# Block-masked attention and two feed-forward layers on one core: three score tiles share a PSUM bank, and the planner of the instruction order judges by three clock moments

## The chip, the cores and the metric

The kernel is one launch on one core of a Trainium2 chip. The metric is the device time of that launch in microseconds (us), median of the runs shown. Five instruction streams run side by side and wait for each other by semaphores: PE (TensorE, matrix products), DVE (VectorE), ACT (ScalarE), POOL (GpSimd) and SP (SyncE, which here only issues DMAs). PSUM is the memory that PE writes its products to; it has eight banks, each of 512 float32 columns on 128 partitions.

## The reference

```python
def _attn_ref(q, k, v):                       # (4, 8, 576, 64), float32
    scores = 1/sqrt(64) * q @ k^T
    scores = where(query_block >= key_block, scores, -1e9)     # blocks of 64 tokens
    scores = scores - max(scores)
    attn = exp(scores);  attn = attn / (sum(attn) + 1e-9)
    return attn @ v

def _moe_ref(x, w_in, w_out):                 # 2304 x 512, d_ff 2048
    h = x @ w_in
    return (max(h, 0) + log1p(exp(-|h|))) @ w_out

def _moe2_ref(x, w_gate, w_val, w_out, rms_g):    # d_ff 1536
    xn = x / sqrt(mean(x * x) + 1e-6) * rms_g
    g = xn @ w_gate
    return (g * sigmoid(g) * (xn @ w_val)) @ w_out

def reference(...):  x = heads merged(attn);  x = _moe_ref(x);  return _moe2_ref(x)
```

## The kernel before

**Attention.** The work is cut into 48 *units* `u`: a batch `b`, a group `g` of 192 query tokens (three blocks of 64, `g` = 0, 1, 2) and a pair `p` of heads. Each unit has three *score tiles* `ib` = 0, 1, 2, one for each block of 64 queries of the two heads (128 rows), and `64 * (3g + ib + 1)` key columns wide, so that the mask costs nothing. For `g = 0`, a unit's first 192 tokens, the three tiles are 64, 128 and 192 columns wide. Units 0, 2, 4, 6, 12 to 15, 24 to 27 and 36 to 39 have `g = 0`, 16 in all. A score tile passes through this chain (`s_tile`, `s_exp`, `s_norm`, then `s_turn` or `s_split`): PE writes the scores into PSUM (L422), DVE takes the row maximum (L627), for the first 12 units scales it (L639), ACT takes the exponential with its row sum (L661), DVE makes the reciprocal of the sum (L669, L670), and the probabilities are normalised. In the first 12 units ("whole" units, float32 products) that is one instruction on POOL (L703), DVE (L704) or ACT (L705), then PE transposes the probabilities into PSUM (L716) and ACT (L722) or DVE (L723) copies them to SBUF. In the other units they are split into two float16 halves (L681 to L688) and a DMA transposes them (L693, `pt<-pst`). At last PE multiplies by v (`pv`), and ACT and DVE write the result as the feed-forward input `x`.

**Feed-forward.** The 2304 tokens are six blocks of 384. All products are in three passes of a split float32 (`PASSES`). `g1` and `g2` are the two products of the first layer, `g34` and `g5` those of the second. Until about 420 us the kernel interleaves attention with nine of the sixteen slices of the first layer for each block, and prepares weights on ACT, DVE and POOL (L448 to L461, L327, L337) as their DMAs land. The rest is feed-forward alone.

**PSUM.** `Banks` hands out whole banks: a score tile, a transposed tile, a `pv` result and a `g1` result each take one of the eight when they are first written and give it back when their last reader is done. `ring_a(u)` is the class from which score tiles and `pv` results come, with room for 4 banks at a time in the first units and 3 after that.

**The order.** Nothing is issued as it stands in the source. Each instruction is recorded by `Plan.op` with its engine, a duration, a key, and the cells that it reads and writes. `Plan.schedule` runs a list schedule with banks, DMAs and a model of PE's clock, whose two speeds change at moments of a fixed grid; `Plan.emit` repeats it with keys drawn towards the latest start of each instruction, keeps the best of 12 orders, and issues all instructions by their planned start. An instruction with alternatives (`aop2`, for instance a copy on ACT or DVE) gets its engine there. The semaphores are set afterwards by the tile layer below, from the tiles that the issued instructions touch, not by the plan.

## Time and profile before

| what | value |
|---|---|
| median of 3 runs | 1040.03 us (1039.77 to 1041.62) |
| the profiled execution | 1040.05 us, of which 1038.3 us span |
| PE, PEld busy | 1009.9 us (97%), 941.9 us (91%) |
| DVE, ACT, POOL busy | 667.8 us (64%), 580.1 us (56%), 214.0 us (21%) |
| the chain that ended last | PE 73%, DVE 9%, ACT 8%, DMA 7% |

The span is the time from the first to the last instruction of the execution that the profiler recorded; 1.75 us of its own time lie around it. PE's busy time includes its pipeline, so the free time of PE is what can be read, not how well its busy time is used. The busy shares are means over stages that differ: in the first 400 us DVE and ACT are busy for three quarters of the time or more, in the last 400 us for a quarter or less.

### The profile page before, as it was taken

How to read it: one execution, taken by the hardware profiler on the slowest of the kernel's cores; microseconds unless marked ns; L12 is line 12 of the kernel's file. 1: busy time of each engine (PE TensorE's matmuls, PEld its weight loads, DVE VectorE, ACT ScalarE, POOL GpSimd, SP SyncE). 2: the span in 40 equal slices, each digit the busy share in tenths (PEclk: the TensorE clock that was granted, in tenths of full speed). 3: DMA queues.
4: the chain of work that ended last, by engine and by line, in shares of the span. 5: the costliest groups of instructions: out<-in, count | busy, mean ns of one | idle time of the engine just before them, and what ended most of it. 6: DMA issues, size and time to landing. Idle time of an engine off the chain costs nothing.

```text
span 1038.3 us, 16885 instructions
## 1 busy us (share of the span) xinstructions
PE 1009.9 (97%) x6136; PEld 941.9 (91%) x6136; DVE 667.8 (64%) x1592; ACT 580.1 (56%) x1352; POOL 214.0 (21%) x289
## 2 busy tenths in 40 slices
PE   5999899999999999999999999999999999999998
PEld 4677898999989999999999999999999999999997
DVE  6899999887888677777888899422422423222322
ACT  6999798777778678877878664211211212111111
POOL 3543433331233023223324342000000000000000
PEclk9999999999999999999999999999999999999999
DMA  7454787958556635456444634200100100000000
GB/s 263 133 194 150 191 196 167 252 116 201 130 132 117 111 102 183 164 209 212 162 158 159 199 102 142 69 1 1 62 1 1 62 1 1 31 1 1 31 1 31
DMA packets 111635, 115.19 MB, mean 111 GB/s; under 512 B 84544, under 2 KB 92352, under 8 KB 110528
## 3 DMA queue, kind: packets, MB, share of 16 engines
q1 hardware_dynamic: 110976, 107.83, 36.8%
q0 software_dynamic: 576, 6.29, 1.6%
q8 instruction: 48, 0.79, 0.3%
q14 instruction: 35, 0.29, 0.1%
HBM read 72.03 MB, written 21.63 MB: 90 GB/s over the span
## 4 chain that ended last, share of the span: by engine, by line
PE 73%; DVE 9%; ACT 8%; DMA 7%; issue 2%; POOL 1%; SPq 0%; POOLq 0%; ACTq 0%; DVEq 0%
PE b L422 73%; DMA pt<-pst 4%; DMA wraw<-in_w_dram 2%; ACT P L661 1%; POOL wa L461 1%; ACT wa L448 1%; DVE wa L456 1%; DVE g L337 1%; ACT w L327 1%; DVE nm L627 1%; DVE wa L458 1%; DVE pst L686 1%; DVE t L836 1%; ACT t L834 1%; ACT P L705 1%
## 5 line engine op out<-in xcount | busy, mean ns | idle before, releaser
L422 PE MATMUL b<-x,w 128*128 128x384 f32 x2880 | 543.6, 338 | 2.0 <-DVE nm L669 0.8
L422 PEld LDWEIGHTS b<-x,w 128*128 128x128 f32 x2880 | 503.8, 188 | 13.8 <-issue 1.3
L422 PE MATMUL b<-g,w 128*128 128x384 f32 x1152 | 229.8, 339 | 2.2 <-DVE g L337 1.9
L422 PEld LDWEIGHTS b<-g,w 128*128 128x128 f32 x1152 | 199.4, 188 | 6.5 <-DVE g L337 3.6
L422 PE MATMUL b<-w,g 128*128 128x512 f32 x648 | 160.4, 392 | 0.0
L932 DVE TENSOR_TENSOR t<-b,t 128x384 f32<-128x384 f32 x72 | 40.0, 556 | 165.3 <-ACT t L931 165.1
L422 PEld LDWEIGHTS b<-w,g 128*128 128x128 f32 x648 | 120.6, 188 | 21.8
L461 POOL TENSOR_TENSOR wa<-wa,wraw 128x512 int32<-128x512 int32 x68 | 95.2, 1401 | 204.0 <-DVE wa L456 119.1
L931 ACT ACTIVATE t<-b 128x384 f32<-128x384 f32 x72 | 35.2, 490 | 171.8 <-PE b L422 171.8
L934 ACT CAST g<-t 128x384 fp32r<-128x384 f32 x72 | 36.8, 513 | 136.4 <-DVE t L933 136.4
L661 ACT ACTIVATE P<-b,nm 128x288 f32<-128x288 f32 (+8 forms) x160 | 80.1, 502 | 16.3 <-DVE nm L639 4.5
L627 DVE TENSOR_REDUCE nm<-b 128x1 f32<-128x288 f32 (+8 forms) x160 | 70.7, 447 | 18.7 <-PE b L422 17.6
L933 DVE TENSOR_TENSOR t<-b,t 128x384 f32<-128x384 f32 x72 | 39.9, 556 | 61.5 <-PE b L422 61.5
L686 DVE SCALAR_TENSOR_TENSOR pst<-P,nm,pst 128x128 f16<-128x128 f32 (+4 forms) x108 | 68.3, 638 | 9.1 <-ACT pst L683 6.7
L422 PE MATMUL b<-khl,qbd 128*128 128x448 f32 (+7 forms) x360 | 68.9, 312 | 1.0 <-ACT pt L722 1.0
L337 DVE TENSOR_TENSOR g<-t,g 128x384 fp32r<-128x384 f32 x96 | 60.5, 632 | 11.4 <-ACT g L327 10.9
L836 DVE SCALAR_TENSOR_TENSOR t<-b,t 128x384 f32<-128x384 f32 x96 | 52.6, 551 | 21.4 <-ACT t L835 21.0
L935 DVE TENSOR_TENSOR g<-t,g 128x384 fp32r<-128x384 f32 x72 | 42.9, 597 | 35.4 <-ACT g L934 35.4
L422 PEld LDWEIGHTS b<-khl,qbd 128*128 128x128 f32 x360 | 57.1, 188 | 3.9 <-ACT pt L722 1.2
L327 ACT CAST g<-t 128x384 fp32r<-128x384 f32 x96 | 49.2, 516 | 19.9 <-DVE t L836 16.8
L448 ACT ACTIVATE wa<-wraw 128x512 f32<-128x512 f32 x68 | 46.1, 678 | 20.9 <-DMA wraw<-in_w2gv_dram 10.7
L833 ACT ACTIVATE t<-b 128x384 f32<-128x384 f32 x96 | 46.5, 493 | 19.1 <-PE b L422 19.0
(91 smaller groups left out, 1055.7 us busy)
## 6 DMA issues: line engine op xcount, KB each, us to landing
wraw<-in_w_dram SPq DMA_DIRECT2D x32, 512.0 KB, 3.6
wraw<-in_w2gv_dram SPq DMA_DIRECT2D x24, 512.0 KB, 3.6
yd<-y SPq DMA_DIRECT2D x12, 768.0 KB, 3.7
y<-yd SPq DMA_DIRECT2D x12, 768.0 KB, 4.5
qf<-in_qP_dram SPq DMA_DIRECT2D x42, 192.0 KB, 2.8
xd<-x SPq DMA_DIRECT2D x4, 1536.0 KB, 7.1
x<-xd POOLq DMA_DIRECT2D x4, 1536.0 KB, 7.4
wraw<-in_w2o_dram SPq DMA_DIRECT2D x12, 512.0 KB, 4.4
```

Source lines behind the costliest of these rows:

```text
L327: "ACT": ("ACT", t_act(n), lambda: nc.scalar.copy(dst(), src())),
L337: "DVE": ("DVE", t_dve(n), lambda: nc.vector.tensor_tensor(dst(), a(), b(), ALU.subtract)),
L422: nc.tensor.matmul(o, lhsT=l, rhs=r, start=start, stop=stop)
L448: op("ACT", t_act(CW), prio, lambda a=a, hv=halves: nc.scalar.activation(a(), hv()[1].bitcast(FP32), ACTF.Abs), [raw], [a])
L461: op("POOL", t_pool2(CW), prio, lambda a=a, hv=halves: nc.gpsimd.tensor_tensor(a().bitcast(I32), a().bitcast(I32), hv()[0].bitcast(I32), A ...
L627: aop("DVE", t_dve(cn), key, lambda sp=sp, col=col, cn=cn: nc.vector.tensor_reduce(nm()[:, col:col + 1], sp()[:, :cn], axis=AX.X, op=ALU.m ...
L661: aop("ACT", 0.24 + cn * 0.836e-3, key, lambda sp=sp, col=col, c0=c0, cn=cn: nc.scalar.activation(P()[:, c0:c0 + cn], sp()[:, :cn], ACTF.E ...
L686: aop("DVE", t_dve(c, True), key, lambda: nc.vector.scalar_tensor_tensor(lo(), pc(), r(), hi(), ALU.mult, ALU.subtract), [P, (P, "pad"), ( ...
L833: op("ACT", t_act(BLK, False), key - 5, lambda: nc.scalar.activation(e(), h()[:, :BLK], ACTF.Abs), [h], [e])
L836: op("DVE", t_dve(BLK), key - 5, lambda: nc.vector.scalar_tensor_tensor(e(), h()[:, :BLK], 0.0, e(), ALU.max, ALU.add), [h, e], [e])
L932: op("DVE", t_dve(BLK), key + 2, lambda: nc.vector.tensor_tensor(u(), ga()[:, :BLK], u(), ALU.mult), [ga, u], [u])
L935: op("DVE", t_dve(BLK), key + 4, lambda: nc.vector.tensor_tensor(g()[:, 1], u(), g()[:, 0].bitcast(FP32), ALU.subtract), [u, (g, 0)], [(g, ...
```

## The change

Three things change. The three score tiles of a `g = 0` unit take one bank together, at columns 0, 64 and 192 (`o0`), where each took a bank of its own. The plan's cells are `(sp, ib)` for every score tile, so that for the plan the three parts of a bank are independent. And `emit` runs 24 rounds instead of 12, judges an order by the mean of its planned end over three places of the clock's grid (`PHASES`) instead of one, and goes on after a round that finds no order.

```diff
-    def schedule(self, key):
+    PHASES = (0.7, 1.8, 2.9)
+
+    def schedule(self, key, phase=PHASES[0]):
...
-                rest, share, dur, z = dur, self.cols[i] / dur, 0.0, t + 0.7
+                rest, share, dur, z = dur, self.cols[i] / dur, 0.0, t + phase
...
-        for r in range(12):
+        for r in range(24):
             try:
                 end, start, ends, bank, choice, eng, took = self.schedule(key)
             except TypeError:
-                break
-            if best is None or end < best[0]:
-                best = (end, start, bank, choice, key)
+                if best is None:
+                    raise
+                key = [(x + y) / 2 for x, y in zip(key, best[4])]
+                continue
+            try:
+                mean = (end + sum(self.schedule(key, p)[0] for p in self.PHASES[1:])) / len(self.PHASES)
+            except TypeError:
+                mean = INF
+            if best is None or mean < best[0]:
+                best = (mean, start, bank, choice, key)
...
+        o0 = (0, 64, 192)[ib] if g == 0 else 0
         for c0, cn in chunks:
-            sp = ring_a(u).new()
+            if g == 0 and ib:
+                sp = packed[u]
+            else:
+                sp = packed[u] = ring_a(u).new()
...
-                    mm(sp()[:, :cn], qt()[:, ib, :], k()[:, c0:c0 + cn], True, True)
+                    mm(sp()[:, o0:o0 + cn], qt()[:, ib, :], k()[:, c0:c0 + cn], True, True)
...
-            aop("PE", ..., key, qk, qr + kr, [sp], ...)
+            aop("PE", ..., key, qk, qr + kr, [(sp, ib)], ...)
...
-            aop("DVE", ... tensor_reduce(..., sp()[:, :cn], ...), [sp], [(nm, ib)])
+            aop("DVE", ... tensor_reduce(..., sp()[:, o0:o0 + cn], ...), [(sp, ib)], [(nm, ib)])
...
-            aop("ACT", ... activation(P()[:, c0:c0 + cn], sp()[:, :cn], ACTF.Exp, ...), [sp, (nm, ib)], ...)
+            aop("ACT", ... activation(P()[:, c0:c0 + cn], sp()[:, o0:o0 + cn], ACTF.Exp, ...), [(sp, ib), (nm, ib)], ...)
```

The whole order is drawn anew, on all engines. Three places follow. In the names `b_125` is a PSUM tile with its number, `y` and `raw` hold k, `qf` and `pst` hold q, `ones` is the identity for the transposes, `P` the probabilities, `nm` the small columns of maxima, sums and reciprocals, `wa` and `wraw` weights in preparation. Line numbers of the changed kernel are 9 to 14 higher (L422 is L431, L627 is L640, L716 is L730). A row ends with the semaphores that the instruction waits for, where they are asked for.

The first is the start of PE's stream with its waits, before (unit 0: 64, 128 and 192 columns; then the first two tiles of unit 1):

```order
L422 MATMUL b_125<-y,qf_107 128x64 [waits DMAHW1_49,DMAHW0_49]
L422 MATMUL b_129<-y,qf_107 128x128
L422 MATMUL b_135<-y,qf_107 128x192
L422 MATMUL b_143<-y,qf_108 128x256 [waits DMAHW2_49]
L422 MATMUL b_158<-y,qf_108 128x320
```

and in the changed kernel:

```order
L431 MATMUL b_125<-y,qf_107 128x64 [waits DMAHW1_49,DMAHW0_49]
L431 MATMUL b_125<-y,qf_107 128x128
L431 MATMUL b_125<-y,qf_107 128x192 [waits DVE_49]
L431 MATMUL b_141<-y,qf_108 128x256 [waits DMAHW2_49]
L431 MATMUL b_156<-y,qf_108 128x320
```

The order is the same, but the third product now waits for DVE: for the maximum of the first part, which reads the same bank. The second place is the start of DVE's stream with its waits, before:

```order
L627 TENSOR_REDUCE nm<-b_125 128x1 [waits PE_49]
L639 TENSOR_SCALAR nm<-nm 128x1 [waits DVE_49]
L627 TENSOR_REDUCE nm<-b_129 128x1 [waits PE_49]
L639 TENSOR_SCALAR nm<-nm 128x1 [waits DVE_49]
L669 TENSOR_SCALAR nm<-nm 128x1 [waits Activation_49]
L627 TENSOR_REDUCE nm<-b_135 128x1 [waits PE_49]
L670 RECIPROCAL nm<-nm 128x1 [waits DVE_49]
```

and in the changed kernel:

```order
L640 TENSOR_REDUCE nm<-b_125 128x1 [waits PE_49]
L652 TENSOR_SCALAR nm<-nm 128x1 [waits DVE_49]
L640 TENSOR_REDUCE nm<-b_125 128x1 [waits PE_49]
L652 TENSOR_SCALAR nm<-nm 128x1 [waits DVE_49]
L683 TENSOR_SCALAR nm<-nm 128x1 [waits Activation_49]
L640 TENSOR_REDUCE nm<-b_125 128x1 [waits Activation_49]
L684 RECIPROCAL nm<-nm 128x1 [waits DVE_49]
```

Again the order is the same; the third maximum now waits for ACT, whose exponentials of the first two parts read the same bank. The third place is PE's stream after the first six score tiles, before:

```order
L716 MATMUL b_198<-ones,P 128x128 x2
L422 MATMUL b_204<-y,pst 128x64
L716 MATMUL b_207<-ones,P 128x128 x2
L422 MATMUL b_212<-y,pst 128x128
L422 MATMUL b_215<-y,pst 128x192
L422 MATMUL b_228<-pt,pst 64x192 x2
L422 MATMUL b_228<-pt,pst 64x64 x2
L716 MATMUL b_257<-ones,P 128x128 x3
L716 MATMUL b_268<-ones,P 128x128 x3
L422 MATMUL b_275<-y,pst 128x256
L422 MATMUL b_284<-y,pst 128x320
L716 MATMUL b_297<-ones,P 128x128
```

and in the changed kernel:

```order
L730 MATMUL b_197<-ones,P 128x128 x2
L730 MATMUL b_204<-ones,P 128x128 x2
L431 MATMUL b_209<-y,pst 128x64
L730 MATMUL b_212<-ones,P 128x128 x3
L431 MATMUL b_219<-pt,pst 64x192 x2
L431 MATMUL b_219<-pt,pst 64x64 x2
L431 MATMUL b_209<-y,pst 128x128
L431 MATMUL b_209<-y,pst 128x192
L431 MATMUL b_235<-y,pst 128x256
L431 MATMUL b_240<-y,pst 128x320
L730 MATMUL b_251<-ones,P 128x128 x3
L730 MATMUL b_282<-ones,P 128x128
```

The transposes of unit 1's second tile (`b_257`, now `b_212`) stand ahead of unit 0's `pv`, and four score products of units 2 and 3 stand between that `pv` and the transposes of unit 1's third tile (`b_268`, now `b_251`). Elsewhere the new order differs in the same manner, by a few matmul groups. Over the first 12 units ACT has two more normalisations of 128x192 (L705), one more of 128x256 and of 128x64, one fewer of 128x320, and in copies of transposed tiles (L722) three fewer of 128x512, two fewer of 128x128 and one more of 128x384.

## Rows read from the trace of the kernel before

**Rows 1.** Windows by stage: busy time of each engine, PEclk, DMA share, GB/s.

```profile
4.38:25.00 20.62, 14.21 (x68) 10.63 (x68) 16.80 (x64) 14.84 (x45) 8.70 (x16) 0.92 0.82 286
25.00:100.00 75.00, 69.97 (x423) 55.26 (x423) 67.67 (x200) 71.60 (x185) 34.89 (x53) 1.00 0.49 157
100.00:420.00 320.00, 312.99 (x2358) 294.07 (x2357) 269.74 (x779) 252.93 (x647) 92.92 (x158) 1.00 0.66 158
420.00:1033.00 613.00, 612.11 (x3291) 581.75 (x3291) 312.90 (x551) 238.87 (x476) 77.08 (x57) 1.00 0.22 74
```

**Rows 2.** Waits of PE from 4 to 25 us: total us, times, longest.

```profile
PE b L716 <- ACT P L705: 3.7, 1, 3.7
PE b L422 <- ACT pt L722: 1.4, 1, 1.4
PE b L716 <- DVE P L704: 1.3, 1, 1.3
```

**Rows 3.** Windows of one us around the fall of PE's clock.

```profile
16.00:17.00 1.00, 0.03 (x1) 0.03 (x1) 1.00 (x9) 0.65 (x2) 1.00 (x1) 0.98 1.10 370
17.00:18.00 1.00, 1.00 (x5) 1.00 (x6) 1.00 (x5) 1.00 (x4) 0.34 (x1) 0.50 1.03 396
20.00:21.00 1.00, 1.00 (x4) 0.70 (x4) 0.64 (x4) 1.00 (x4) 0.77 (x2) 0.81 0.27 107
```

**Rows 4.** Timeline of unit 0's maxima and exponentials: start, us, engine, line.

```profile
5.52 0.31 ACT L661 ACTIVATE P<-b,nm 128x64 f32<-128x64 f32 x1 [3.50 <-DVE nm L639]
5.61 0.29 DVE L627 TENSOR_REDUCE nm<-b 128x1 f32<-128x128 f32 x1
...
6.25 0.36 DVE L627 TENSOR_REDUCE nm<-b 128x1 f32<-128x192 f32 x1
...
6.83 0.42 ACT L661 ACTIVATE P<-b,nm 128x192 f32<-128x192 f32 x1 [0.25 <-DVE nm L639]
...
8.35 1.49 PE L422 MATMUL b<-y,qf 128*128 128x384 f32 x2
```

**Rows 5.** Timeline of the events that the new order moves, 12 to 24 us.

```profile
12.15 0.39 ACT L722 COPY pt<-b 128x256 f32<-128x256 f32 x1
...
16.97 1.54 PE L716 MATMUL b<-ones,P 128*128 128x128 f32 x6 [3.71 <-ACT P L705]
...
21.48 1.09 PE L422 MATMUL b<-pt,pst 128*64 128x192 f32 x12
...
23.50 0.62 ACT L661 ACTIVATE P<-b,nm 128x384 f32<-128x384 f32 x1
```

**Rows 6.** ACT's groups by shape, first 100 us: count, busy us, mean ns, idle before.

```profile
L722 ACT COPY pt<-b 128x512 f32<-128x512 f32 x10 | 6.1, 609 | 0.0
L722 ACT COPY pt<-b 128x384 f32<-128x384 f32 x7 | 3.5, 496 | 0.7 <-PE b L716 0.7
L705 ACT ACTIVATE P<-P,nm 128x320 f32<-128x320 f32 x4 | 2.3, 578 | 0.9 <-DVE nm L669 0.9
L722 ACT COPY pt<-b 128x128 f32<-128x128 f32 x8 | 2.1, 266 | 1.0 <-PE b L716 1.0
L705 ACT ACTIVATE P<-P,nm 128x256 f32<-128x256 f32 x1 | 0.5, 548 | 0.0
L705 ACT ACTIVATE P<-P,nm 128x192 f32<-128x192 f32 x1 | 0.5, 461 | 0.0
L705 ACT ACTIVATE P<-P,nm 128x64 f32<-128x64 f32 x1 | 0.4, 351 | 0.0
```

**Rows 7.** Waits of PE from 25 to 100 us.

```profile
PE b L716 <- ACT P L661: 1.0, 2, 0.6
...
PE b L422 <- ACT P L661: 0.6, 1, 0.6
```

**Rows 8.** Waits of PE from 100 to 420 us.

```profile
PE b L422 <- DMA pt<-pst: 2.9, 5, 0.9
...
PE b L422 <- ACT P L661: 0.6, 2, 0.3
```

More of the change, by code (lines that the diff above doesn't have):

```diff
@@ L590, in small @@
         aop2([e[k] for k in kind], key, reads, writes, False)
-    part = {}
+    part, packed = {}, {}
     def s_tile(u, ib, key, after):
@@ L616, in qk @@
                 if whole(u):
-                    mm(sp()[:, :cn], qt()[:, ib, :], k()[:, c0:c0 + cn], True, True)
+                    mm(sp()[:, o0:o0 + cn], qt()[:, ib, :], k()[:, c0:c0 + cn], True, True)
                     return
                 for m, (a, c) in enumerate(PASSES):
-                    mm(sp()[:, :cn], d[:, a, ib, :], khl[p][:, c, c0:c0 + cn], m == 0, m == 2)
+                    mm(sp()[:, o0:o0 + cn], d[:, a, ib, :], khl[p][:, c, c0:c0 + cn], m == 0, m == 2)
             if c0 == 0:
                 qk_op.append(len(plan.ops))
-            aop("PE", max(0.213, 0.006 + cn * 1.667e-3) if whole(u) else 3 * t_mm(cn), key, qk, qr + kr, [sp], after=after, cols=t_mm16((4 if whole(u) else 3) * cn))
+            aop("PE", max(0.213, 0.006 + cn * 1.667e-3) if whole(u) else 3 * t_mm(cn), key, qk, qr + kr, [(sp, ib)], after=after, cols=t_mm16((4 if whole(u) else 3) * cn))
         for c, (sp, (c0, cn)) in enumerate(zip(bank, chunks)):
             col = ib + c
-            aop("DVE", t_dve(cn), key, lambda sp=sp, col=col, cn=cn: nc.vector.tensor_reduce(nm()[:, col:col + 1], sp()[:, :cn], axis=AX.X, op=ALU.max, negate=True), [sp], [(nm, ib)])
+            aop("DVE", t_dve(cn), key, lambda sp=sp, col=col, cn=cn: nc.vector.tensor_reduce(nm()[:, col:col + 1], sp()[:, o0:o0 + cn], axis=AX.X, op=ALU.max, negate=True), [(sp, ib)], [(nm, ib)])
         if len(chunks) == 2:
@@ L654, in s_exp @@
         nm, done = part[u]
+        o0 = (0, 64, 192)[ib] if units[u][1] == 0 else 0
         P = part[u, ib] = R_P.new()
@@ L660, in s_exp @@
             col = 4 + ib + c
-            aop("ACT", 0.24 + cn * 0.836e-3, key, lambda sp=sp, col=col, c0=c0, cn=cn: nc.scalar.activation(P()[:, c0:c0 + cn], sp()[:, :cn], ACTF.Exp, scale=scale, bias=nm()[:, ib:ib + 1], accum_out=nm()[:, col:col + 1]), [sp, (nm, ib)], [P, (nm, "s", ib)])
+            aop("ACT", 0.24 + cn * 0.836e-3, key, lambda sp=sp, col=col, c0=c0, cn=cn: nc.scalar.activation(P()[:, c0:c0 + cn], sp()[:, o0:o0 + cn], ACTF.Exp, scale=scale, bias=nm()[:, ib:ib + 1], accum_out=nm()[:, col:col + 1]), [(sp, ib), (nm, ib)], [P, (nm, "s", ib)])
         if len(chunks) == 2:
```

## The prediction

> **What bounds the kernel now.** I read the windows by stage first, to see where PE is free at all [rows 1]. From 420 us to 1033 us PE idles 613.00 - 612.11 = 0.9 us, so that nothing that an order does there can show. From 100 to 420 us it idles 320.00 - 312.99 = 7.0 us, with DVE busy for 84% and ACT for 79%. From 25 to 100 us it idles 75.00 - 69.97 = 5.0 us, and there ACT is busy for 71.60 of 75.00 us: that stretch goes at ACT's pace. From the first product at 4.38 us to 25 us it idles 6.4 us. So at most some 19 us, 1.9% of the time, can be won, and only by an order under which PE waits less; the amount of PE's work is the same before and after. I then read who ends PE's waits in each stretch. Early it is three single waits, 3.7, 1.4 and 1.3 us, all for one tile's chain of maximum, exponential, normalisation and copy [rows 2]. Behind the longest of them PE's granted clock shows 0.50, the lower of its two levels, 1.2 of 2.4 GHz: 0.98 in the slice from 16 us, 0.50 at 17, 0.81 in the slice from 20, so (1 - 0.98)/0.5 + 3 + (1 - 0.81)/0.5 = 3.4 us at half speed, a loss of 1.7 us of work [rows 3]. Later the waits are many and small, the largest group 2.9 us in five for transposing DMAs [rows 8].
>
> **The change, part by part.** The first thing is what the shared bank does to the issued waits, since the plan takes the three parts as independent and the tile layer below does not: the third product of unit 0 now waits for the first maximum, the third maximum for two exponentials, as the order's rows with their waits show, and the exponentials in turn wait for the maxima issued ahead of them. I follow unit 0 by hand with the durations of before.
>
> Before, the second maximum starts at 5.61 us and the third at 6.25 [rows 4]. Now the first maximum can start only when the second product is done, at 5.61; it takes 0.22 (0.29 and 0.36 for 128 and 192 columns, 0.07 for each 64), the third product follows at about 5.9, and since it can no longer overlap the second one I give it 0.85 to its reader where the rows show 0.64 between the readers. The second maximum then runs at 6.75 to 7.04, the first exponential at 7.1 instead of 5.52, the second to about 7.95, the third maximum at 8.0, and after its scaling the third exponential at 8.7 instead of 6.83. The transposes of the first two tiles, which stand ahead of the 384-column product in PE's stream, go with them: that product starts at 9.6 instead of 8.35. **The new waits cost PE 1.25 us at this point.**
>
> Then the new order gains it back. The copy that the first `pv` waits for starts at 12.5 instead of 12.15 [rows 5]. The six transposes that were held until 16.97 are parted: three of them (unit 1's second tile, now normalised on POOL) are done ahead of that `pv`, the score products of units 2 and 3 fill 1.5 us of the hole, and the other three start at about 16.3. Unit 1's `pv` starts at about 20.9 instead of 21.48. So PE is about 0.6 us ahead there. ACT is not: going on through its new order, the 384-column exponential of unit 3 starts at about 25.2 instead of 23.50, and of these 1.7 us only 0.461 + 0.351 = 0.8 us are normalisations that it has done earlier than before [rows 6]. As the next stretch goes at ACT's pace, the bounds are -0.6 (PE's lead is kept) and +1.7 (ACT's lag lands on PE); I take **+0.4**, between the lead and the true lag of 0.9. The clock: my chain still leaves PE idle from 15.0 to 16.3 and from 16.8 to 19.7, so I expect the lower level once more, a little later, at the same price: 0, with -1.7 as the bound if it does not fall.
>
> From 25 to 100 us ACT's load changes by the engine choices. Normalisations: 2 x 0.461 + 0.548 + 0.351 - 0.578 = +1.24 us. Copies: -3 x 0.609 - 2 x 0.266 + 0.496 = -1.87 us [rows 6]. Two of the normalisations are counted above, so 1.87 - (1.24 - 0.81) = 1.4 us less remain for this stretch; the copies go to DVE, which is busy for 67.67 of 75 us [rows 1] and takes most of that room away. I take **-0.5**, bounds -1.4 and 0.
>
> Units 4 and 6 have shared banks in this stretch too. Their order is three products, three maxima, three exponentials, so the first exponential waits for two more maxima, 0.29 + 0.36 = 0.65 us each [rows 4]. Other work may fill it: **+0.6**, bounds 0 and +1.3. The other twelve units stand after 100 us, where DVE is busy for 269.74 of 320 us and ACT for 252.93 [rows 1]. Each can lose about one exponential to a waiting maximum or the reverse, 0.42 [rows 4]; the room on both engines and the many matmuls that stand between a unit's scores and its `pv` cover it. I take **0**, bounds 0 and, if half of them show, 6 x 0.42 = +2.5.
>
> What the freed banks give: PE's waits that end with an exponential are those for a score bank to come free (the exponential is a score tile's last reader), 1.0 + 0.6 + 0.6 = 2.2 us [rows 7, 8]. A third of the score tiles are packed: **-0.7**, bounds -2.2 and 0. The new criterion redraws the order everywhere else; where the waits of 100 to 420 us fall next is open, and I take 0, bounded by the largest group, the transposing DMAs, gone or come twice, 2.9 us either way [rows 8]. Rounds and phases cost no instruction.
>
> Sum: 0.4 - 0.5 + 0.6 + 0 - 0.7 + 0 = -0.2 us on the profiled execution's own 1040.05 (1038.3 span and 1.75 around it), which lies 0.02 above the median of the runs shown: **1039.9 us**.
>
> A row of before cannot show two engines at one bank, since no two tiles share one there [rows 4]: maximum and exponential of neighbouring tiles overlap freely (the 128-column maximum starts 0.09 us after the 64-column exponential). The Trainium skill ("PSUM — Partial Sum Buffer", section "PSUM bank collisions raise a hardware error") says that two engines must be kept apart by bank and not by address, reads against reads included. By that rule the three parts never overlap on different engines in any of the 16 units, and the time would be that of the slower rival below; by the rows' overlap taken as still possible, that part of the sum would be 0.
>
> **The rivals.**
> *The shared bank costs more than the order gives.* Place: ACT in the first 100 us, ACT and DVE after that. All of ACT's lag lands on PE (+1.7), both of units 4 and 6 lose their 0.65 (+1.3), half of the later units 0.42 each (+2.5), and the lighter ACT gives its 0.5: 1040.05 + 5.0 = 1045.0. For it: the plan knows nothing of these waits, and ACT has 3.4 us of room in 75 [rows 1]. Against it: in the later units the maxima and exponentials are already issued nearly in sequence, and after 100 us both engines have room. It decides when over 2.6 of these 5.5 us land.
> *The early hole closes.* The three early waits are 6.4 us together [rows 2]; if the parted transposes halve them (-3.2) and the clock then stays up (-1.7): 1035.1. For it: more work stands in the hole. Against it: by my chain the hole only moves.
> *The banks were the limit.* All 2.2 us of bank waits go, and ACT's 1.4 us count in full: 1036.4. For it: ACT paces 75 us. Against it: the waits are five small ones, and an order kept under a looser rule need not spend the freedom there.
> *The change does nothing that shows*: gains and losses cancel; this is my forecast.
>
> **How the numbers follow.** A measurement of this kernel can tell about 0.2%, 2.1 us, from no change. Forecast, within 2.1 us: 0.42, with a range of its own of 1038 to 1042. Slower rival: 0.28. Early hole: 0.14. Banks: 0.16. The last two make 0.30 for faster. The range reaches over most of the three rivals: 1035.0 to 1045.3; about half of the early hole's cases and a third of the slower rival's lie outside, together some 0.17.
>
> **What would show it.** Right: the 64-, 128- and 192-column exponentials at about 7.1, 7.5 and 8.7 us; the 384-column product near 9.6; unit 1's `pv` between 20.5 and 21.5; a stretch at 0.50 as long as before, beginning a few us later; PE idle of about 5 us from 25 to 100 and 7 from 100 to 420. Wrong: exponentials of unit 0 near 5.5 to 6.9 (the bank costs nothing); no slice at 0.50 before 30 us; PE idle from 25 to 100 above 7 (slower) or below 3 (faster); new waits of PE's score products for DVE or ACT of over 1 us anywhere; waits for transposing DMAs far from 2.9 us, which would say that the new order and not the bank decides.

## The result, and the profile of the changed kernel

The changed kernel takes 1046.93 us (median of 6 runs, 1046.01 to 1050.08), the kernel before 1040.29 us (6 runs, 1039.19 to 1041.62). The ratio is 1.0065, interval 1.0052 to 1.0079: 6.6 us slower, and outside the predicted range. The profiled execution took 1046.88 us, of which 1045.0 us are span.

The windows by stage of the changed kernel, and below them its three stretches at half speed (columns as in [rows 1]):

```profile
4.38:25.00 20.62, 16.13 (x72) 10.64 (x74) 17.20 (x58) 14.91 (x46) 10.01 (x19) 0.83 0.80 283
25.00:100.00 75.00, 69.13 (x418) 54.94 (x415) 66.47 (x203) 68.56 (x174) 29.78 (x41) 0.95 0.45 151
100.00:420.00 320.00, 312.23 (x2328) 294.40 (x2327) 268.06 (x771) 249.03 (x645) 101.62 (x169) 0.98 0.67 158
420.00:1033.00 613.00, 611.26 (x3289) 581.58 (x3288) 319.25 (x552) 240.02 (x484) 86.24 (x63) 1.00 0.22 75
17.44:24.27 6.83, 5.14 (x23) 3.44 (x24) 6.49 (x24) 6.03 (x17) 4.12 (x8) 0.50 0.46 155
41.34:48.16 6.82, 6.07 (x24) 3.73 (x24) 5.97 (x23) 6.61 (x20) 1.64 (x4) 0.50 0.48 163
116.43:126.67 10.24, 8.71 (x48) 8.36 (x43) 7.51 (x36) 7.66 (x25) 3.86 (x9) 0.50 0.53 140
```

PE's idle time has hardly changed: 4.5 us (6.4 before), 5.9 (5.0), 7.8 (7.0) and 1.7 (0.9) by stage, 19.9 us against 19.3. What has grown is its busy time, 1016.5 us over the whole span against 1009.9, for the same products. Where it grew is in the last three rows: the granted clock shows 0.50 three times instead of once, and PE is busy in these stretches for 5.14 + 6.07 + 8.71 = 19.9 us, against 3.4 us before [rows 3]. Half of that is 10.0 us, against 1.7. The first reading is therefore that the clock is the loss. The experiments below show that most of the loss is something else.

Unit 0's chain came as it was worked out. ACT's and DVE's rows at its start (start, duration, and in brackets the idle time before, with what ended it) answer to [rows 4]:

```profile
7.22 0.31 ACT L675 ACTIVATE P<-b,nm 128x64 f32<-128x64 f32 x1 [5.19 <-DVE nm L640]
7.52 0.36 ACT L675 ACTIVATE P<-b,nm 128x128 f32<-128x128 f32 x1
8.58 0.42 ACT L675 ACTIVATE P<-b,nm 128x192 f32<-128x192 f32 x1 [0.61 <-DVE nm L652]
...
6.89 0.29 DVE L640 TENSOR_REDUCE nm<-b 128x1 f32<-128x128 f32 x1 [0.91 <-PE b L431]
8.00 0.36 DVE L640 TENSOR_REDUCE nm<-b 128x1 f32<-128x192 f32 x1 [0.20 <-ACT P L675]
```

The exponentials start at 7.22, 7.52 and 8.58 us (worked out: 7.1, 7.5, 8.7), the second maximum at 6.89 (6.75). No maximum and exponential of the unit run at the same time any more. That is what the rule of the Trainium skill ("PSUM — Partial Sum Buffer", section "PSUM bank collisions raise a hardware error") asks for, and the trace agrees with it; but here semaphores keep the two apart, so no run shows what the hardware would do without them.

PE's waits by stage (who was waited for; us in total, times, longest), which answer to [rows 2, 7, 8]: from 4 to 25 us, from 25 to 100 us, and from 100 to 420 us.

```profile
PE b L730 <- ACT P L719: 3.8, 2, 3.5
...
PE b L730 <- ACT pt L736: 2.2, 5, 0.7
PE b L730 <- ACT P L675: 1.2, 1, 1.2
...
PE b L431 <- ACT P L675: 0.7, 2, 0.5
...
PE b L431 <- DMA pt<-pst: 2.6, 3, 0.9
PE b L431 <- DVE x L797: 1.4, 1, 1.4
PE b L431 <- ACT khl L556: 1.2, 1, 1.2
PE b L431 <- ACT P L675: 1.0, 3, 0.7
```

The early hole has only moved (3.5 us for one normalisation instead of 3.7). From 25 to 100 us the transposes wait five times, 2.2 us in all, for ACT's copies of transposed tiles. Before, PE waited nearly as long for them there, 0.4 us ahead of a transpose and 1.6 ahead of other products:

```profile
PE b L422 <- ACT pt L722: 1.6, 3, 1.0
```

New near 120 us is a wait of 1.4 us for an addition of DVE (L797), and one of 1.2 us of a score product for ACT's part of k (L556).

### The profile page after: what moved, and what is told of

It is laid out like the page before. It is cut to its first block, busy times and chain, and to the rows that moved or that the text cites. A ratio compares the mean times of both kernels' runs of the same rounds, so it can differ in the third digit from the quotient of the medians.

```text
span 1045.0 us, 16874 instructions
## 1 busy us (share of the span) xinstructions
PE 1016.5 (97%) x6136; PEld 948.2 (91%) x6136; DVE 673.4 (64%) x1585; ACT 576.0 (55%) x1350; POOL 228.1 (22%) x298
## 4 chain that ended last, share of the span: by engine, by line
PE 73%; DVE 5%; DMA 4%; ACT 3%; issue 1%; POOL 1%; POOLq 0%; ACTq 0%; DVEq 0%; SPq 0%
PE b L431 73%; DMA pt<-pst 2%; DMA wraw<-in_w_dram 1%; DVE wa L465 1%; POOL wa L470 1%; ACT wa L457 1%; DVE wa L461 1%; ACT t L848 0%; DVE wa L467 0%; DVE t L850 0%; ACT w L336 0%; ACT g L336 0%; DMA wraw<-in_w2o_dram 0%; DVE g L346 0%; DMA wraw<-in_w2gv_dram 0%
## 5 line engine op out<-in xcount | busy, mean ns | idle before, releaser
L431 PE MATMUL b<-x,w 128*128 128x384 f32 x2880 | 545.6, 338 | 1.3 <-DVE x L767 0.5
L431 PEld LDWEIGHTS b<-x,w 128*128 128x128 f32 x2880 | 505.2, 188 | 12.5 <-ACT P L675 1.2
L431 PE MATMUL b<-g,w 128*128 128x384 f32 x1152 | 228.3, 340 | 0.4 <-DVE g L346 0.4
L431 PEld LDWEIGHTS b<-g,w 128*128 128x128 f32 x1152 | 200.3, 188 | 3.5 <-DVE g L346 0.6
L431 PE MATMUL b<-w,g 128*128 128x512 f32 x648 | 161.2, 393 | 0.0
L431 PEld LDWEIGHTS b<-w,g 128*128 128x128 f32 x648 | 120.6, 188 | 21.5
L640 DVE TENSOR_REDUCE nm<-b 128x1 f32<-128x288 f32 (+8 forms) x160 | 70.8, 450 | 23.4 <-PE b L431 18.5
L431 PE MATMUL b<-khl,qbd 128*128 128x448 f32 (+7 forms) x360 | 70.5, 319 | 2.6 <-ACT khl L556 1.2
L431 PEld LDWEIGHTS b<-khl,qbd 128*128 128x128 f32 x360 | 58.6, 196 | 5.9 <-ACT P L675 1.8
L847 ACT ACTIVATE t<-b 128x384 f32<-128x384 f32 x96 | 46.4, 489 | 18.4 <-PE b L431 18.1
```

Of the source, the lines that this page charges most:

```text
L431: nc.tensor.matmul(o, lhsT=l, rhs=r, start=start, stop=stop)
L640: aop("DVE", t_dve(cn), key, lambda sp=sp, col=col, cn=cn: nc.vector.tensor_reduce(nm()[:, col:col + 1], sp()[:, o0:o0 + cn], axis=AX.X, o ...
L847: op("ACT", t_act(BLK, False), key - 5, lambda: nc.scalar.activation(e(), h()[:, :BLK], ACTF.Abs), [h], [e])
```

## The experiments

Three theories at the start. **A, the clock:** the holes of the new order make it fall twice more, and half of the busy time at 0.50 is the loss. **B, the shared banks:** the waits between maximum and exponential cost the time themselves. **C, the order:** an order drawn anew is worse, with or without shared banks. One point needs no run. Built with the shared banks and the old criterion (12 rounds, one phase), the kernel has the same instructions in the same order on PE, DVE and ACT as the changed one. So the new criterion decides nothing here: the shared banks give the plan another order, and the old criterion finds the same one.

### Is it the clock?

Both kernels once more, unaltered.

> The changed kernel once more, nothing altered, for a second profile. The moments at which the granted clock can change stand at another distance from the first instruction in each execution. Theory A (half-speed stretches make the loss): again two or three stretches at 0.50 behind the holes near 17, 40 and 115 us, and a time that follows them: 1046 to 1050 us with 8 to 11 us of PE work lost or stretched, less only if a stretch is missing. Theory B (the waits at the shared banks): 1046 to 1048 whatever the clock does.

> The kernel before once more, nothing altered, for a second profile. Theory A: one stretch at 0.50 near 17 us and 1039 to 1041 us; should a second stretch stand near 113 us, as in the same order with packed tiles, then 1041 to 1043. Theory B says nothing of a second stretch: 1039 to 1041.5 with or without one.

They took 1046.01 and 1039.36 us, one execution each. The windows by stage of the second profile of the changed kernel, and its stretches at 0.50:

```profile
4.38:25.00 20.62, 15.57 (x78) 10.41 (x79) 17.20 (x59) 15.25 (x47) 9.98 (x19) 0.92 0.80 285
25.00:100.00 75.00, 67.11 (x409) 53.37 (x408) 66.13 (x202) 67.60 (x172) 29.83 (x41) 0.98 0.46 151
100.00:420.00 320.00, 311.26 (x2330) 293.24 (x2329) 268.36 (x772) 249.53 (x646) 102.00 (x169) 0.99 0.68 158
...
19.62:23.03 3.41, 3.41 (x18) 2.10 (x17) 3.29 (x12) 3.34 (x9) 1.32 (x4) 0.50 0.43 145
46.93:50.34 3.41, 3.41 (x15) 2.48 (x14) 1.23 (x7) 2.73 (x8) 1.29 (x1) 0.50 0.18 32
118.61:125.43 6.82, 5.03 (x28) 4.68 (x28) 4.82 (x25) 5.37 (x19) 2.22 (x6) 0.50 0.38 91
```

PE is busy at 0.50 for 11.9 us instead of 19.9, so by theory A 4.0 us should come back. The execution is 0.9 us faster. The rest went into idle time: 5.0 + 7.9 + 8.7 = 21.7 us in these three stages, against 18.1 in the first profile. PE's rows of the same transposes, in the first profile and in the second, show how:

```profile
45.58 1.12 PE L730 MATMUL b<-ones,P 128*128 128x128 f32 x4
46.90 0.91 PE L730 MATMUL b<-ones,P 128*128 128x128 f32 x3 [0.21 <-ACT pt L736]
...
50.19 0.49 PE L730 MATMUL b<-ones,P 128*128 128x128 f32 x3
```

```profile
43.61 0.66 PE L730 MATMUL b<-ones,P 128*128 128x128 f32 x4
46.14 0.55 PE L730 MATMUL b<-ones,P 128*128 128x128 f32 x3 [1.87 <-ACT pt L736]
...
50.39 0.49 PE L730 MATMUL b<-ones,P 128*128 128x128 f32 x3
```

In the second profile PE comes to the four transposes 2.0 us earlier, at full speed, and then waits 1.87 us for ACT's copy. In the first it comes late, at half speed, and waits 0.21 us. At 50.2 and 50.4 us both are at the same instruction. Here half speed took the place of a wait, and cost nothing.

The Trainium skill ("TensorE: Matmul & The Clock Gate", section "HAM oscillation — how this bites in real kernels") counts half of the time at the lower clock as lost. The two traces here disagree, 4.0 us by the rule and 0.9 us measured; where PE had nothing to wait for, a later run agrees (the stretch at 595 us below).

The second profile of the kernel before says the same. Its stretch at 0.50 is twice as long (15.32 to 22.15 us, PE busy for 5.31 us), and it is 0.7 us faster than the first. Next, PE's holes filled with work that nobody needs: in the changed kernel ahead of unit 14's first score product and of unit 2's first transpose, and in the kernel before 12 products ahead of the transposes of unit 1's second tile. Their results are overwritten by the products that follow.

```diff
+                for _ in range({(14, 0): 5}.get((u, ib), 0)):
+                    mm(sp()[:, :128], ones, ones, True, True)
...
+            for _ in range({(2, 0): 12}.get((u, ib), 0)):
+                mm(o()[:, :128], ones, ones, True, True)
```

> The changed kernel in its own order, with 12 extra 128x128 products of the identity with itself just ahead of the transpose that ends the hole from 15.6 to 19.1 us, and 5 just ahead of unit 14's first score product, which waited in the hole near 114 us. Their results are overwritten by the real products, so they add only PE work, and only where PE waited. Theory A (the clock): the changed kernel is slower because PE's clock falls three times, each time behind a hole; with the first and third hole filled those two stretches at 0.50 go and the one from 41 to 48 us stays; half of the PE time in them, (5.1 + 8.7) / 2 = 6.9 us, comes back less up to 1 us for the added products: 1039 to 1042 us. Theory B (the waits at the shared banks cost the time themselves, on DVE and ACT): added products remove no such wait: 1046 to 1048 us. Theory C (the new order leaves PE idle more): the same as B, or later by the added products, 1047 to 1050.

> The kernel before in its own order, with 12 such products ahead of the transpose that ends its hole from 13.3 to 17.0 us. Theory A: the one stretch at 0.50, from 17.0 to 20.4, goes, and 1.7 us with it: about 1038.5 us, a granted clock of 1.0 up to 60 us. Theories B and C: added work that hides nothing: 1040.3 to 1042 us.

> The kernel before with the 12 added products once more, for a second profile. Its first profile had the stretch at 0.50 earlier, not gone, and gained 2 us between 200 and 350 us and 0.8 us after 420 us instead. If that gain belongs to the kernel, PE's idle time from 100 to 420 us is again near 5.2 us and the time near 1037.5; if it was that execution's, near 7 us and 1039 to 1040.

The changed kernel with added products: 1045.92 us (4 runs, ratio 1.0059, 1.0044 to 1.0074). The early stretch at 0.50 is gone, the second halved, the third still 6.8 us; PE is busy at 0.50 for 9.0 us. By theory A 5.4 us should return, less up to 1 us for the added products; the median is 1.0 us lower.

The kernel before with added products: 1037.66 us (10 runs, ratio 0.9974, 0.9965 to 0.9983), faster than both kernels, and 1037.45 in one more execution. Theory A had given 1038.5, but not for the right reason. The windows of one stretch in the first profile and of another in the second:

```profile
14.08:17.49 3.41, 3.41 (x17) 3.41 (x18) 3.28 (x13) 1.56 (x5) 2.58 (x2) 0.50 1.05 368
```

```profile
113.16:116.58 3.42, 3.34 (x11) 3.28 (x11) 3.04 (x12) 2.27 (x7) 0.15 (x1) 0.50 0.65 162
```

The stretch at 0.50 did not go. It stands among the added products in one profile and 100 us later in the other, and the times agree within 0.2 us. What both profiles share is less waiting later: PE waits for transposing DMAs for 0.9 and 0.6 us from 100 to 420 us, against 2.9 before [rows 8]. By the start times of the same products, PE is 0.2 to 0.7 us late at 250 us and 2 us early at 350. Why a handful of useless products at 14 us does that is not settled.

**Theory A falls as the main cause:** in the first 130 us of these kernels the clock falls where PE waits anyway. The clock is not free everywhere, though. In a run further down (the first repair in the changed kernel's order) it also falls at 595.45 us, where PE is busy throughout. That stretch, and PE's rows around it in the changed kernel and in that run:

```profile
595.45:598.86 3.41, 3.41 (x11) 3.16 (x10) 3.13 (x5) 2.86 (x5) 1.75 (x2) 0.50 0.54 160
```

```profile
595.25 8.99 PE L431 MATMUL b<-x,w 128*128 128x384 f32 x49
...
595.28 8.99 PE L435 MATMUL b<-x,w 128*128 128x384 f32 x40
```

Both begin together, but in 8.99 us PE does 49 products in the one and 40 in the other. From 600 us to the end the same products are 1.6 us later, close to half of 3.41. Over all executions on record, kernel by kernel, a mean clock lower by 0.001 goes with some 0.35 us more (an estimate, a line through 184 executions). The changed kernel's six have a mean clock of 0.990, the kernel before 0.996 (78 executions), so about 2 of the 6.6 us may go with the clock; that it causes them is not shown. The rest is not the clock: the last run below has a mean clock of 0.994, PE is busy at 0.50 for 8.2 us in its profile against 3.4 in that of the kernel before, 2.4 us even at half of the difference, and it is 5.8 us slower.

### Is it the shared banks?

The kernel before, with its own order on every engine, instruction for instruction; only the PSUM tiles change. After the plan is made, the three tiles of a unit are put into one bank where one is free for the whole life of the three (`spot` gives that bank's columns from 0, 64 or 192).

```diff
+        for home, parts in self.homes:
+            s = [start[i] for x in parts for i in x.users]
+            lo, hi = min(s), max(s)
+            ok = [k for k in [x.bank for x in parts] + list(range(8)) if all(y < lo or x > hi for x, y in stay.get(k, []))]
...
-                    mm(sp()[:, :cn], qt()[:, ib, :], k()[:, c0:c0 + cn], True, True)
+                    mm(spot(u, ib, sp)(cn), qt()[:, ib, :], k()[:, c0:c0 + cn], True, True)
```

> The kernel before with its own order on every engine, instruction for instruction, but with the three score tiles of 11 of the 16 units of the first 192 tokens (0, 2, 4, 13, 14, 15, 27, 36 to 39) laid into one bank at the same three column places as in the changed kernel; the planner knows nothing of it. So it has the new waits and not the new order. Theory B (the waits cost the time): most of the loss shows, 1044 to 1047, and DVE's and ACT's waits at these units grow. Theory A: the first products of unit 0 come some 1.2 us later, its hole moves or grows by no more than that, and the clock falls once as in the kernel before: 1040 to 1042.5; it can only be higher with a second stretch at 0.50. Theory C: no new order, no loss: 1040 to 1041.

> The kernel before in its own order, with the three tiles of unit 0 alone in one bank. Theory B for unit 0: its exponentials start at about 7.2, 7.5 and 8.6 us instead of 5.5, 6.2 and 6.8, PE's lag is 1.3 to 1.8 us at 30 us and stays, since the stretch up to 100 us goes at ACT's pace: 1041.6 to 1042.2 us, if no second stretch at 0.50 comes with it. Theories C and D: 1040.5 us.

> The kernel before in its own order, with the three tiles of units 2 and 4 alone in one bank each. Theory B for the early units (maxima and exponentials wait for each other at one bank where ACT sets the pace, so the delay stays): the exponentials from 28 us on are 0.8 to 1.8 us late and PE's work with them up to 100 us, 1041.3 to 1042.5 us. If the early part of the eleven units' loss was only the execution's: 1040.2 to 1041 us.

> The kernel before in its own order, with the three tiles of the eight units 13, 14, 15, 27 and 36 to 39 in one bank each. With unit 0 alone at no loss and eleven units at 3.3 us, what the early units do not take must show here. Theory B for the late units (a maximum waits for the exponential before it at the same bank, and the next exponential for it, where DVE sets the pace near 115 us): 1041.5 to 1043 us, PE's lag between 115 and 130 us 1 to 2 us. If the early units are the whole of it: 1040.3 to 1041.

| units with one bank, order of before | median | ratio to the kernel before, run beside it |
|---|---|---|
| 0 | 1041.19 us (11 runs) | 1.0003 (0.9994 to 1.0013) |
| 2, 4 | 1041.48 us (12 runs) | 1.0002 (0.9992 to 1.0013) |
| 13, 14, 15, 27, 36 to 39 | 1042.12 us (12 runs) | 1.0018 (1.0005 to 1.0030) |
| all these eleven | 1043.63 us (5 runs) | 1.0030 (1.0017 to 1.0044) |

Unit 0 alone is the clearest. Its exponentials are as late as in the changed kernel, 1.8 us:

```profile
7.29 0.32 ACT L692 ACTIVATE P<-b,nm 128x64 f32<-128x64 f32 x1 [5.26 <-DVE nm L658]
...
8.65 0.42 ACT L692 ACTIVATE P<-b,nm 128x192 f32<-128x192 f32 x1 [0.61 <-DVE nm L670]
```

and nothing of it is left in the time: PE's products are 0.9 us late at 8 us and 0.2 at 15, so that the hole behind takes it. The early units together cost 0.5 us by their ratios, within what can be measured; the eight later ones 1.9 us (0.5 to 3.1). All eleven cost 3.1 us (1.8 to 4.6). What PE waits for more is the later units' transposing DMAs; with all eleven, from 100 to 420 us (2.9 us before, 3.9 with the eight later ones alone):

```profile
PE b L439 <- DMA pt<-pst: 5.0, 9, 1.7
```

**Theory B holds at the order of before, for 3.1 us, about half of the 6.6**, and its place is the later units rather than the first ones. In the profiles of all four rows but the first a second stretch at 0.50 also stands near 114 us; what part of the cost is its doing is not separated. How much the same waits cost in the new order is not measured.

### Is it the order alone?

The new criterion with a bank for each tile; and the changed kernel with shared banks only for the twelve units after the first 90 us (`if g == 0 and ib and u > 6`). Both draw an order of their own.

> The kernel before with the new criterion alone (24 rounds, mean over three phases), each score tile in a bank of its own. Its order differs from both kernels on every engine. Theory A: the time follows the idle time of PE plus half of PE's busy time at 0.50, whatever the order: 1037 to 1044, with no more than two stretches at 0.50 if it is below 1043. Theory B: no shared bank, so no loss: 1038 to 1041. Theory C (a redrawn order is the loss): 1044 to 1048.

> The changed kernel with the three tiles in one bank only for the 12 units after the first 90 us; units 0, 2, 4 and 6 keep a bank for each tile. The order is drawn anew and differs from both kernels. Theory A: no relation to the number of packed units; the time is what PE's idle time and half its busy time at 0.50 give, 1037 to 1048. Theory B: the early waits are gone, and if these cost the time, 1040 to 1042. Theory C (any order but that of before is worse, as it was with no tile packed at all): 1044 to 1048.

They took 1045.33 us (4 runs, ratio 1.0047, 1.0031 to 1.0064) and 1047.88 us (4 runs, 1.0071, 1.0054 to 1.0088). So theory C holds too: this order, drawn anew, costs 4.9 us without a single shared bank. Where it loses them is not settled: PE idles 19.5 us in the four stages (19.3 before) and is busy at 0.50 for 16.1 us instead of 3.4. PE's and ACT's longest waits of the second kernel, from 110 and from 100 to 122 us, show what an order can do:

```profile
PE b L431 <- DVE t L850: 5.8, 1, 5.8
...
ACT wa L457 <- DMA wraw<-in_w_dram: 2.1, 3, 1.6
```

ACT stands before weights that have not landed, while PE waits 5.8 us in one piece. That the one comes of the other is not shown by these rows; the next runs test it.

### One place in ACT's stream

In the changed kernel the same stands near 119 us. ACT's rows, and DVE's:

```profile
119.18 0.67 ACT L457 ACTIVATE wa<-wraw 128x512 f32<-128x512 f32 x1 [0.81 <-DMA wraw<-in_w_dram]
119.74 0.65 ACT L458 ACTIVATE wraw<-wraw 128x512 int32<-128x512 uint32 x1
120.29 0.49 ACT L336 CAST g<-t 128x384 fp32r<-128x384 f32 x1
...
120.82 0.56 DVE L346 TENSOR_TENSOR g<-t,g 128x384 fp32r<-128x384 f32 x1 [2.52 <-ACT g L336]
121.30 0.41 DVE L797 SCALAR_TENSOR_TENSOR x<-b,dsc,x 128x192 fp32r<-128x192 f32 x1
```

A pair that starts a weight slice waits 0.81 us for its DMA and takes 1.3 us; the cast of `g` stands behind it, DVE waits 2.52 us for that, the addition into `x` stands behind DVE's `g`, and PE's `pv` waits for the addition. In the kernel before the pair stands seven places behind the cast:

```profile
109.48 0.51 ACT L327 CAST g<-t 128x384 fp32r<-128x384 f32 x1
...
112.89 0.68 ACT L449 ACTIVATE wraw<-wraw 128x512 int32<-128x512 uint32 x1 [0.45 <-DMA wraw<-in_w_dram]
```

**Theory D:** this place is the loss from 100 to 130 us. First the test in the kernel before: its own order, with only that pair moved ahead of the cast.

```diff
+        first, second = max((x for x in self.pairs if start[x[0]] < 130), key=lambda x: start[x[0]])
...
+        ahead = sorted((i for i in range(n) if self.ops[i][0] == "ACT" and start[i] < start[first]), key=lambda i: (start[i], i))
...
+        start[first], start[second] = start[ahead[-8]] + 1e-6, start[ahead[-8]] + 2e-6
         for i in sorted(range(n), key=lambda i: (start[i], i)):
             self.ops[i][3]()
```

> The kernel before, its banks and its order, but with the weight pair of ACT that stands at 112.9 us put ahead of the cast of g at 109.5 us, as in the changed kernel. Its DMA lands at 112.5 to 112.9 us whatever ACT does. Theory D: ACT stands still for up to 3.3 us, the cast of g starts near 114 us instead of 109.5, DVE and PE wait behind it, PE's lag at 130 us is 2 to 4 us, 1042 to 1045 us. Theory A: only if a second stretch at 0.50 appears. Theories B and C (shared banks, a wholly new order): nothing of either is in this kernel, 1040.3 us.

It took 1045.16 us (5 runs, ratio 1.0044, 1.0031 to 1.0058), 4.6 us more. The waits of ACT and DVE from 98 to 132 us, and PE's row behind them, first in the kernel before and then in this one:

```profile
ACT wraw L455 <- DMA wraw<-in_w_dram: 3.8, 1, 3.8
...
DVE nm L675 <- ACT P L667: 4.5, 1, 4.5
...
111.05 0.46 PE L422 MATMUL b<-ones,am 128*128 128x128 f32 x2
...
116.09 0.80 PE L427 MATMUL b<-ones,am 128*128 128x128 f32 x2 [4.29 <-ACT P L667]
```

Two instructions of ACT in the wrong place are enough for two thirds of what the change lost. A second stretch at 0.50 did appear (113.69 to 120.52 us), which theory A had made its condition. But the delay is the wait's: PE's products are 0.7 us late ahead of it, 4.9 behind it, 5.6 while half speed lasts and 4.8 after that. Then the repairs in the changed kernel, its own order kept: the pair behind the cast (`start[first] = start[second] = start[behind[3]] + 1e-6`); a bank of its own for each tile of units 0 and 2 and for two single tiles of later units (four by the expectations below), wherever that order leaves one free; and both.

> The changed kernel in its own order but for two instructions: the pair of ACT that begins a weight slice near 119 us (absolute values and low bits, 128x512, which waits for the slice's DMA) stands behind the cast of g and three exponentials instead of ahead of them. What it makes is read by DVE only 40 us later. Theory D (ACT's stream: the pair waits 0.8 us for its DMA and takes 1.3 us, and the cast of g, DVE's instruction behind it, which waits 2.3 to 2.5 us, and the pv product, which waits 1.4 to 1.6 us, all stand behind it): DVE's wait falls below 1 us, the wait of the pv product below 0.5 us, the lag of PE's work behind the kernel before at 130 us falls by 1.5 to 3.5 us, 1043.5 to 1045.5 us. Theory A (only the clock): a change only so far as the stretch at 0.50 near 117 us goes; if it stays, 1046 to 1047. Theory B (same-bank waits): 1046 to 1047.

> The changed kernel in its own order, instruction for instruction, but the tiles of 128 and 192 columns of units 0 and 2, and four single tiles after 185 us, stand in banks of their own, wherever that order leaves a bank free for a tile's whole life. So unit 0 loses its new waits: its exponentials start at about 5.5, 6.2 and 7.0 us and the product of 384 columns near 8.4 instead of 9.7. Theory A: the first hole shifts by a micro-second or so, the holes near 40 and 115 us stay, and so do their stretches: 1044.5 to 1047. Theory B: the largest of the new waits (1.3 us at unit 0) is gone, 1043 to 1045. Theory C (the order itself): 1046 to 1047.

> The changed kernel in its own order, with both repairs: the tiles of units 0 and 2 (and four single ones after 185 us) in banks of their own, and the weight pair near 119 us behind the cast of g. Theory D together with the early same-bank waits: unpacking alone brought 2.4 us up to 100 us, which the wait near 117 us took back; with that wait gone both show: 1041 to 1043.5 us. Theory D without them: as with the second repair alone, 1043.5 to 1045.5. Theory A: 1044 to 1047, by the number of stretches at 0.50.

They took 1047.98 us (5 runs, ratio 1.0066, 1.0053 to 1.0078), 1047.31 (4 runs, 1.0065, 1.0050 to 1.0080) and 1047.40 (5 runs, 1.0066, 1.0054 to 1.0079): no gain. In the first one's profile (1048.43 us) PE's products are 1.1 us ahead of the changed kernel at 130 us and still 1.0 at 420; there the stretch at 595 us, shown above, then takes 1.6. The wait at the cast is gone all the same. With the pair moved, DVE's wait for `g` from 112 to 126 us:

```profile
DVE g L350 <- ACT g L340: 0.2, 1, 0.2
```

PE's row of that `pv`, and SP's issues ahead of it:

```profile
120.94 0.85 PE L435 MATMUL b<-pt,vhl 128*64 128x192 f16 x12 [1.11 <-DVE nm L689]
...
114.03 0.33 SPq L445 DMA_DIRECT2D wraw<-in_w_dram  x1
115.34 0.33 SPq L445 DMA_DIRECT2D raw<-in_vP_dram  x1
115.76 1.25 SPq L712 DMA_TRANSPOSE pt<-pst  x1
```

And the time from the issue to the landing of that transposing DMA alone:

```profile
DMA to landing us min/median/max: 5.0/5.0/5.0
```

DVE's 2.5 us are 0.2, but the `pv` starts only 0.8 us earlier, at 120.94, 0.2 us after the transposing DMA has landed (115.76 + 5.0). The row puts the wait down to a small DVE instruction, but its end goes with the DMA's landing: the `pv` also starts at most 0.2 us after it with units 0 and 2 unpacked (landing 5.8 us after the issue) and with both repairs (5.2). In the kernel before that DMA lands 3.5 us after its issue, with no weight load close ahead. **Theory F** puts it down to the load of the weight slice ahead of it, which is not needed for 40 us. So, with the pair behind sixteen more instructions, that load goes behind the transposing DMA:

```diff
+        load = max((i for i in self.loads if start[i] < start[first]), key=lambda i: start[i])
+        start[load] = min(start[i] for i in self.turns if start[i] > start[load]) + 1e-6
```

> The changed kernel in its own order, with the weight pair of ACT near 119 us behind the cast of g and fifteen instructions more, and with that slice's weight load, issued at 114.3 us, put behind the transposing DMA that SP issues at 116.0 us. Theory F (with the pair moved, the next limit is that transposing DMA: it lands 4.4 to 5.8 us after its issue, where the kernel before shows 3.5, and in all runs with the pair moved the pv product starts 0.1 us after it lands; the weight load is in its way): it lands 3.3 to 4.0 us after its issue, the pv product starts 0.8 to 1.5 us earlier than 120.9 us, the lag of PE's work at 130 us falls from 6.3 to between 4.8 and 5.8 us, 1044.5 to 1046.5 us. Theory A (the clock): 1046 to 1048, unless the stretch at 0.50 near 117 us goes. If the transposing DMA stays at 4.5 us or more without the weight load, it is the values' load ahead of it or the transposition itself: 1046.5 to 1048.

> The same with units 0 and 2 unpacked as well. Theory F with the early same-bank waits: another 1 to 2.4 us less, 1042.5 to 1045 us, lag at 130 us of 3 to 4.5 us. Theory F alone: as without unpacking, 1044.5 to 1046.5. Theory A: 1046 to 1048.

They took 1047.18 us (5 runs, ratio 1.0061, 1.0047 to 1.0075) and 1046.54 (6 runs, 1.0052, 1.0036 to 1.0068). The DMA still lands 4.5 us after its issue in both, and in the first the `pv` starts 0.1 us after that. The unaltered changed kernel, with the weight load ahead, shows 4.9 and 4.4 us in its two profiles, so nothing is left for theory F. At last both repairs with PE's holes filled as above:

> The changed kernel in its own order with all three repairs: units 0 and 2 unpacked, the weight pair near 119 us behind the cast of g, and the added products in PE's holes near 15 and 113 us (12 and 5 of 128x128, overwritten by the real ones). The hole near 40 us stays. Theory E (no single cause: each hole that is closed leaves the next one, and a stretch at 0.50 stands behind each dense group of holes): with the holes near 15 and 113 us closed the stretches near 17 and 117 us go, the one near 41 us stays, 1042 to 1044.5 us. Theory A alone: the same, with the time following the stretches. Theory B or D alone: no gain over the two repairs without products, 1046.5 to 1048.

1046.21 us (5 runs, ratio 1.0056, 1.0042 to 1.0070). PE is busy at 0.50 for 8.2 us instead of 19.9, and the time is 0.7 us lower: once more the clock is not the main cause. Theory E's forecast, 1042 to 1044.5, was wrong with it.

## Why the prediction was wrong, step by step

**The step that failed** is the last one of the sum: "The new criterion redraws the order everywhere else; where the waits of 100 to 420 us fall next is open, and I take 0, bounded by the largest group, the transposing DMAs, gone or come twice, 2.9 us either way." The size was taken from the waits that the old order had, and it was put at nothing. An order redrawn without any shared bank costs 4.9 us. It was also put down to the wrong part of the change: with shared banks the old criterion finds the same order, so it is the banks that redraw it. A new order can bring waits that the old one kept short, such as ACT standing before a weight slice that has not landed, with DVE and PE behind it: one such place costs 4.6 us in the kernel before, where the slice lands 4.5 us after its issue. By these two runs a bound had to allow for 4 to 5 us. In the changed kernel the same place brought no gain when it was repaired, so which of its waits make up its loss stays open.

**The twelve later units** were taken at 0 with +2.5 as the bound, because DVE and ACT have room there on average. At the order of before eight of them cost 1.9 us (0.5 to 3.1). The mechanism was named, but the room on DVE and ACT did not cover it; the value taken was that of the wrong end.

**Unit 0 and the first 25 us** were right in mechanism and in most times: the exponentials; the 384-column product at 9.67 us (9.6); the copy ahead of the first `pv` at 11.79 (12.5); unit 1's `pv` at 20.79 (20.9); the 384-column exponential of unit 3 at 24.42 (25.2). The price of +0.4 is within what was measured for unit 0 alone at the order of before, 0.3 us (-0.6 to 1.4).

**The clock** was expected to fall "once more, a little later, at the same price". It fell three times, and the count was wrong. The price of the further stretches is small where PE would wait (8 us less at 0.50 gave 0.9 us) and full where it would not (1.6 us for 3.4).

**Units 4 and 6**, +0.6: units 2 and 4 cost 0.2 us (-0.8 to 1.4) at the old order, so nothing speaks against the term; unit 6 was packed in no run at that order.

**ACT's lighter load**, -0.5: ACT did get lighter by more than that, 68.56 us busy against 71.60, but PE did not gain. It idles 5.9 us there instead of 5.0, with nearly the same 2.2 us (2.0) for ACT's copies. "That stretch goes at ACT's pace" did not hold in the sense that less work on ACT makes it shorter; why is not shown.

**The freed banks**, -0.7: PE's waits that end with an exponential grew, from 2.2 us [rows 7, 8] to 1.2 + 0.7 us up to 100 us and 1.0 from 100 us.

**From 420 us on**, where "nothing that an order does there can show", PE idles 1.7 us instead of 0.9, most of it in one wait of 1.3 us near 594 us for DVE. And most of the signs of being right came (the exponentials, PE's idle time of 5.9 and 7.8 us, 2.6 us for transposing DMAs) in a kernel that is 6.6 us slower: half speed had largely taken the place of idle time, so PE's idle time was a poor sign.

The rival on the slower side was the right one in sign and, as far as it was measured, in one of its three places (the later units; the first 100 us cost 0.5 us, within the noise). It was 1.9 us short (1045.0 against 1046.9), and that it came so close is partly luck, since it held the order itself at no cost.

**What stays open.** At the old order the shared banks cost 3.1 us; that leaves some 3.5 us for the new order, a difference and not a measurement, and some 2 us of the whole may go with the clock. None of the seven repairs of the changed kernel lowered its median by more than 1.0 us, though the aimed-at wait was gone or shorter in most. Where rows were read the next wait stood close behind. Which chain holds the changed kernel in the end is not settled.

## What to carry to other kernels

When a change makes a planner draw its order anew, price the new order as a loss of its own: find in each in-order stream the instructions that wait for a transfer, and ask what it costs if one of them comes to stand ahead of work that another engine needs; two instructions of ACT did 4.6 us here. Before a stretch at half speed is booked as a loss, look whether PE would wait behind it: a second profile of the same kernel, with the clock's falls elsewhere, helps to tell (1.6 us for 3.4 where it would not wait, 0.9 for 8 where it would). And a repair that removes the wait it aims at without moving the time says that the next wait stood right behind; follow the DMA's landing, since the name that the wait carries can be that of another instruction.

## What was not expected of the hardware

The stretches at 0.50 stand at other places in each profile of one program (16.96 or 15.32 us in the kernel before; 14.08 or 113.16 us with added products) and are 3.4, 6.8 or 10.2 us long, with times of the two profiles that agree within 0.9 us. A transposing DMA of the same size landed 3.5 us after its issue in the kernel before and 4.4 to 5.8 us with loads of weights and values issued within 2 us ahead of it, 4.5 us with the values' load alone; what makes the difference is not shown. And twelve useless products made the kernel before 2.7 us faster, by less waiting some 300 us behind them.
